# Early values loads, copies behind the products, and the MLP's first step ahead of the last early chunk

## The chip, the cores and the metric

One core of one Trainium2 chip runs the whole program. The metric is the device time of one execution in microseconds (us); less is better. The times shown are the median of three runs, and one further execution was taken with the hardware profiler.

## The reference

A gated linear attention feeds two MLPs one after the other. Cut to what matters:

```python
for t in range(S):                       # B=4, H=8, S=768, D=48
    state = alpha[:, :, t, :, None] * state + einsum('bhd,bhe->bhde', k[:, :, t], v[:, :, t])
    y[:, :, t] = einsum('bhd,bhde->bhe', q[:, :, t], state)
x = y.transpose(0, 2, 1, 3).reshape(B * S, H * D)      # 3072 x 384
x = silu(x @ w_in) @ w_out                             # 384 -> 2048 -> 384
out = (silu(x @ w_gate) * (x @ w_val)) @ w2_out        # 384 -> 1536 -> 384
```

The weights come as 64-bit floats; the kernel decodes them to 32 bits on the chip.

## The kernel before, in words

**Attention by chunks.** The sequence is cut into 24 chunks of 128 tokens (NCH; chunk n is batch n % 4, position n // 4), each with 8 heads in four pairs. Two pairs are a "duo" d, so chunk n has duos 2n and 2n+1. For a chunk VectorE runs a scan over the decays (`scan_r`, line 418), a reciprocal and a second scan (`scan_g`, line 431); GpSimd multiplies keys and queries by them (line 443, two products per chunk, named kq); TensorE makes the scores (`scores2`, line 455); VectorE masks them (`mask2`, line 469, into one of three `pt` buffers), ScalarE copies the keys (`keys2`, line 476); and TensorE makes the values product `pv` (line 638). For the first four chunks (n < NE = 4) `pv` has a second kind of matmul (line 659), which reads a rearranged copy of the values, `v3`, that lies in the tile `start`; `spread` (line 682, the copy on line 686) writes it on GpSimd. There are two such copies, used in turn.

**Early chunks.** Chunks 0 to 6 (NF = 7) are done by `early(m)` (line 482). Its calls set the order on each engine, which is the order in the program: scores of chunk m, `pv` of chunk m-1, masks and keys of chunk m, `chunk_high(m - 1)`, `spread(m)`, the scans and products of chunk m+2, from chunk 3 on a weight unit decoded by VectorE in a PSUM bank (`early_unit`, line 381), `chunk_end(m - 1)`, guards (squares summed on ScalarE, line 579), and loads of raw weights. Loads are issued on SP: `scan_g` ends with the load of the input of two chunks on, `chunk_end` with the values load `load_v(n + 2)` (line 405; two buffers). Fillers (line 609) are matmuls into a bank that nobody reads.

**The first MLP by blocks.** Tokens form seven blocks; block 0 is chunks 0 to 3 (512 columns), block 1 chunks 4 to 6 (384 columns). A step (j, f) of block j has a first-layer product `g1` (line 828, nine matmuls, with weight unit 2f), the Silu on ScalarE and a subtraction for the low part on VectorE (`act1`, line 835), and a second-layer product `g2` (line 855, unit 2f+1). Every unit is split into a high part (ScalarE, line 804) and a low part (VectorE, `sub`, line 322), since each product is made from high and low parts. Units 4 and on are decoded by `units1` (line 1372) in three VectorE instructions (lines 93, 98, 103) that are called between the steps. The list `turns` (line 1446) interleaves the steps of blocks 0 and 1; the main loop (line 1557) issues `g1` of step s+1 ahead of `g2` of step s. Ahead of it stand the last `pv` (chunk 6, `attn(1, False)`, line 1549), `open_late` (line 346: memsets on GpSimd and four copies on ScalarE, lines 351 to 360), the first `g1` and its Silu.

```python
        if m:
            pv(m - 1)
...
        if m < NE:
            spread(m)
        if m + 2 < NF:
            scan_r(m + 2, 0, NP)
            scan_g(m + 2, 0, NP)
```

After the first MLP (blocks 2 to 6 carry the other chunks' attention along) the second MLP follows; the change does not touch it.

Of the kernel before, what the change touches and what calls it, by code (L numbers as in the profile page):

```python
# [23 lines left out]
NCH = B * NC  # L24
# [244 lines left out]
def fast(ctx, tc, pk, w1, w2, out, bad_i):  # L269
# [5 lines left out]
    blocks1, n = [], 0  # L275
# [91 lines left out]
    in_t, raw_in, v_t, r_t = {}, {}, {}, {}  # L367
# [4 lines left out]
    NE, NF = B, len(blocks1[0]) + len(blocks1[1])  # L372
# [30 lines left out]
            load_in(later_in.pop(0)[1])  # L403

    def load_v(n):
        if n >= NCH:
            return
        v_t[n] = ap.tile([128, NP, C], F32, tag="in_v", name=f"in_v{n}")
        SP.dma_start(
            out=v_t[n], in_=pk[n, :, A_W + 2 * W:].rearrange("p (r e) -> p r e", r=NP)  # L410
        )
# [19 lines left out]
    def scan_g(n, i, k):  # L431


        rg, cs = rg4[n % 2], slice(i * CA, (i + k) * CA)
        DVE.tensor_tensor_scan(
            out=rg[:, 1, cs], data0=in_t[n][0][:, cs],
            data1=rc4[:, i:i + k].rearrange("p i t -> p (i t)"), initial=0.0, op0=ALU.mult, op1=ALU.add,
        )
        by_pair = rg.rearrange("p x (i t) -> p x i t", i=NP)
        for lo in range(i, i + k, 2):  # L440
            d = (n * NP + lo) // 2
            kq_t[d] = kqs[d % 6]
            (DVE if d == 0 else POOL).tensor_tensor(
                out=kq_t[d][:, :, :2 * C].rearrange("p i (x t) -> p x i t", x=2),
                in0=in_t[n][1][:, :, lo:lo + 2], in1=by_pair[:, :, lo:lo + 2, 1:], op=ALU.mult,
            )
        c, b = divmod(n, B)
        if c:
            for p in range(i, i + k):
                t = state[b][:, p]  # L450
                ACT.activation(out=t, in_=t, func=AF.Copy, scale=by_pair[:, 0, p, 0:1])
        if i + k == NP:
            load_in(n + 2)
# [28 lines left out]
    def early(m):  # L482

        if m == 0:
            yd_place(0)
        s = {}
        for d in (2 * m, 2 * m + 1):
            filler(max(m - 1, 0), 4 if d == 1 else 1)  # L490
            s[d] = scores2(d)
        if m:
            pv(m - 1)
        for d in s:
            mask2(d, s[d])
            keys2(d, s[d])
            if m == 0:
                (scan_r if d == 0 else scan_g)(1, 0, NP)
        if m:
            chunk_high(m - 1)  # L500
            yd_place(m)
        if m < NE:
            spread(m)
        if m + 2 < NF:
            scan_r(m + 2, 0, NP)
            scan_g(m + 2, 0, NP)
        if m >= 3:
            early_unit(yd_t[m][:, 512:])
        if m:
            chunk_end(m - 1)  # L510
        up_to("gd", 2 * m, guard, ND)
        up_to("l1", 2 * m + 1, load1, NU1)
# [91 lines left out]
    def yd_place(n):  # L604

        t = yd_t[n] = banks((6, 2)[(NF - 1 - n) % 2] if n < NF else 6, f"yd{n}")
        y_t[n] = t[:, 256:768]
# [30 lines left out]
    def pv(n):  # L638

        c, b = divmod(n, B)
        v = v_t[n]
        if n >= NF:
            yd_place(n)
        y = y_t[n]
        first, last = n * NP, n * NP + NP
        heads = [(p, h, slice(64 * h, 64 * h + 64)) for p in range(NP) for h in range(2)]
        pts = [pt_t.pop(g) for g in range(first, last)]
        for p, h, hs in heads:  # L650
            if n < NE and p == 0:
                continue
            cs, r = slice(p * C, p * C + C), half(p, h)
            PE.matmul(  # L654
                y[r:r + 64, cs], v[:, p, hs], pts[p][:, h], start=p in (n < NE, 2), stop=True,
                skip_group_check=True,
            )
            if n < NE:
                PE.matmul(
                    y[r:r + 64, cs], v3[n % 2][:, p - 1, hs], pts[0][:, h], start=False, stop=True,  # L660
                    skip_group_check=True,
                )
        if c < NC - 1:
            ds = ds_t[n] = yd_t[n][:, 768:768 + NP * D].rearrange("p (r e) -> p r e", r=NP)
            for p, h, hs in heads:
                PE.matmul(
                    ds[hs, p], kt_t[first + p][:, hs], v[:, p, 64 * h:64 * h + D],
                    start=False, stop=True, skip_group_check=True,
                )
            for g in range(first, last):  # L670
                kt_t.pop(g)
        if c:
            for p, h, hs in (heads[2 * p + h] for p in (0, 2, 1, 3) for h in range(2)):
                r = half(p, h)
                PE.matmul(
                    y[r:r + D, p * C:p * C + C], state[b][hs, p],
                    kq_t[(first + p) // 2][(hs, p % 2, slice(C, 2 * C)) if n < NF else (hs, 1, p % 2)],
                    start=False, stop=True,
                    skip_group_check=True,
                )  # L680

    def spread(n):


        t = v3[n % 2].rearrange("p k (h x) -> p k h x", h=2)
        POOL.tensor_copy(
            t[:, :, :, D:],
            v_t[n][:, 0].rearrange("p (h x) -> p h x", h=2)[:, :, :D].rearrange(
                "p h (k r) -> p k h r", k=KT
            ),  # L690
        )
# [136 lines left out]
    def g1(s):  # L828
        j, f = steps[s]
        w = len(blocks1[j]) * C  # L830
        h_t[j, f] = bank(s % 2, f"h{j}_{f}")[:, :w]
        xk = [(x_t[j][:, 0, k, :w], x_t[j][:, 1, k, :w]) for k in range(KT)]
        product(h_t[j, f], unit_t["1", 2 * f], xk)
# [494 lines left out]
    def attn(lag=1, more=True, first=None):  # L1328
        done, new = st["pv"], None
        if st["qk"] - st["pv"] * NP >= NP + lag - 1:  # L1330
            pv(done)
            st["pv"] += 1
        if more and st["qk"] < NG:
            new = st["qk"]
            qkt(new)
            st["qk"] += 1
        rest = first and first()
        if new is not None:
            d, odd = divmod(new, 2)
            ahead, top = d + 3, ND  # L1340
            causal(new)
            keys(new)
        if rest:
            rest()

        if st["pv"] > done:
            chunk_high(done)
            chunk_end(done)
        if new is None:
            return  # L1350
        if odd:
            up_to("a3", ahead, stage_a3, top)
            up_to("b", d + 2, stage_b, ND)
        else:
            up_to("a1", ahead, stage_a1, top)
            up_to("c", d + 1, stage_c, ND)
            up_to("a2", ahead, stage_a2, top)
            up_to("gd", d - 1, guard, ND)
        begin_later()
# [12 lines left out]
    def units1(ahead=4, top=NU1):  # L1372

        up_to("s1", st["h1"] - 1, lambda u: low_unit(("1", u), DVE), NU1)
        up_to("h1", st["f1"] - 1, lambda u: high_unit(("1", u), wp, "w"), NU1)
        up_to("e1", st["d1"] - 1, lambda u: decode_unit(("1", u), 1), NU1)
        up_to("d1", st["d1"], lambda u: decode_unit(("1", u), 0), min(top, st["l1"]))
        up_to("f1", st["e1"] - 1, lambda u: decode_unit(("1", u), 2), NU1)
        up_to("l1", st["d1"] + ahead - 1, load1, NU1)
# [63 lines left out]


    FB = 8
    turns = [(0, 0), (0, 1)]
    for k, n in enumerate((2, 2, 2, 2, 3, 3, 2)):
        f1 = sum(j for j, _ in turns)
        turns += [(1, f1 + i) for i in range(n)] + [(0, k + 2)] * (k + 2 < FB)
    steps = turns + [(0, f) for f in range(FB, NF1)]  # L1450
    steps += [(j, f) for j in range(2, NB1) for f in range(NF1)]

    due, n = [first] * (2 * len(turns)), first
# [92 lines left out]
    first_d = first // 2  # L1546
    need1(1)
    units1()
    attn(1, False)
    up_to("gd", first_d - 1, guard, ND)  # L1550
    estack.close()
    open_late()
    g1(0)
    rest = act1(*steps[0])
    units1()
    rest()
    for s, (j, f) in enumerate(steps):
        need1(2 * f + 1)
        if s == 0:
            units1()  # L1560
        n = 19 + 2 * (s + 3 - len(steps))
        if s + 1 < len(steps):
            need1(2 * steps[s + 1][1])
            if n >= 19:
                run(OUTPUT[n] - PAIR)
            g1(s + 1)
        slot(s, 0, (lambda: act1(*steps[s + 1])) if s + 1 < len(steps) else None)
        if n >= 19:
            if s + 1 < len(steps):
                free_banks.append((s + 1) % 2)  # L1570
            run(OUTPUT[min(n + 1, 23)] - PAIR)
        g2(j, f)
        slot(s, 1)

    wstack.close()
    free_banks += [2, 3, 4]
# [90 lines left out]
```

## Time and profile before

| | us |
|---|---|
| Median of 3 runs | 943.12 |
| Lowest and highest run | 943.05, 945.03 |
| The profiled execution's own time | 947.71 |
| Its span in the trace | 946.0 |
| TensorE (PE) busy | 905.8 (96%) |
| VectorE (DVE) busy | 611.6 (65%) |
| ScalarE (ACT) busy | 451.4 (48%) |
| GpSimd (POOL) busy | 279.4 (30%) |

The span is what the trace covers; the execution's own time has 1.7 us around it, and stands 4.6 us above the median of the runs without a profile. Busy shares are means over the whole span. SP issues most of the transfers, and SPq, ACTq are the queues' issues. PEld is TensorE's loading of weights, which overlaps its matmuls.

### The profile page before, as it was taken

The page shows a single profiled execution, that of the slowest core. Times are in us where ns is not written, and L with a number is a line of the kernel's source. Part 1 is how long each engine was busy: PE and PEld are TensorE (multiplying, and loading weights), DVE is VectorE, ACT ScalarE, POOL GpSimd, SP SyncE. Part 2 cuts the span into 40 slices and gives each one's busy share as a digit, 9 for nine tenths or more (in the row PEclk, how much of TensorE's full clock was granted, in tenths as well). Part 3 has the DMA queues.
Part 4 walks back from the last instruction along what each step waited for, and adds up shares of the span by engine and source line. Part 5 has one row for each costly group of instructions (what it writes and reads, how often), then busy time and mean ns, then how long its engine had stood idle before and what let it go on. Part 6 is the DMA issues. An engine that isn't in the chain of part 4 may idle for free.

```text
span 946.0 us, 14403 instructions
## 1 busy us (share of the span) xinstructions
PE 905.8 (96%) x5261; PEld 771.9 (82%) x5261; DVE 611.6 (65%) x1079; ACT 451.4 (48%) x1005; POOL 279.4 (30%) x389
## 2 busy tenths in 40 slices
PE   7569999999999999999999999999999999999996
PEld 4458998889999998888888888878888878888785
DVE  7569966556767577466258457786467875577732
ACT  1355544555556465455446444453454444444432
POOL 5311004528868789677318200000000000000000
PEclk8789999999999999999999999999999999999998
DMA  6665301233564465542466466632557513855301
GB/s 214 203 216 200 118 1 66 84 124 116 181 205 143 155 198 169 177 131 103 134 220 226 173 234 224 242 117 84 201 211 284 188 34 118 283 180 220 134 1 70
DMA packets 43007, 150.89 MB, mean 160 GB/s; under 512 B 4400, under 2 KB 9008, under 8 KB 40240
## 3 DMA queue, kind: packets, MB, share of 16 engines
q1 hardware_dynamic: 42304, 149.30, 46.3%
q8 instruction: 43, 0.70, 0.3%
q10 hardware_dynamic: 624, 0.59, 0.2%
q14 instruction: 36, 0.29, 0.1%
HBM read 118.03 MB, written 29.88 MB: 156 GB/s over the span
## 4 chain that ended last, share of the span: by engine, by line
PE 86%; DVE 3%; issue 3%; DMA 2%; POOL 2%; ACT 2%; SPq 1%; ACTq 0%; POOLq 0%
PE o L1257 15%; PE h L823 6%; PE x L872 6%; PE x L873 6%; PE x L875 6%; PE h L824 6%; PE h L826 6%; PE D L1194 5%; PE A L1194 5%; PE E L1194 5%; PE yd L654 3%; PE K L1194 2%; PE B L1194 2%; PE G L1194 2%; PE H L1194 2%
## 5 line engine op out<-in xcount | busy, mean ns | idle before, releaser
L322 DVE TENSOR_TENSOR gl<-h,gh 128x384 fp32r<-128x384 f32 (+1 forms) x112 | 68.5, 612 | 90.9 <-ACT h L841 85.6
L872 PE MATMUL x<-gh,w 128*128 128x384 f32 (+1 forms) x336 | 121.2, 361 | 4.3 <-DVE x1e L881 2.2
L823 PE MATMUL h<-x,w 128*128 128x384 f32 (+1 forms) x336 | 122.6, 365 | 1.8 <-DMA x<-y 1.6
L873 PE MATMUL x<-gh,w 128*128 128x384 f32 (+1 forms) x336 | 120.8, 360 | 0.0
L824 PE MATMUL h<-x,w 128*128 128x384 f32 (+1 forms) x336 | 120.8, 359 | 0.0
L840 ACT ACTIVATE gh<-h 128x384 fp32r<-128x384 f32 (+1 forms) x112 | 59.9, 535 | 101.1 <-PE h L826 99.7
L1257 PE MATMUL o<-gh,ring 128*128 128x512 f32 x288 | 88.7, 389 | 0.0
L875 PE MATMUL x<-gl,w 128*128 128x384 f32 (+1 forms) x336 | 84.5, 359 | 0.0
L826 PE MATMUL h<-x,w 128*128 128x384 f32 (+1 forms) x336 | 84.3, 358 | 0.0
L872 PEld LDWEIGHTS x<-gh,w 128*128 128x128 f32 x336 | 63.1, 188 | 10.6 <-DVE x1e L881 2.7
L823 PEld LDWEIGHTS h<-x,w 128*128 128x128 f32 x336 | 63.1, 188 | 10.6 <-issue 5.4
L531 POOL TENSOR_TENSOR kq<-in,r 128x256 f32<-128x256 f32 x34 | 33.7, 990 | 118.6 <-DVE r L520 118.6
L873 PEld LDWEIGHTS x<-gh,w 128*128 128x128 f32 x336 | 63.1, 188 | 5.2
L824 PEld LDWEIGHTS h<-x,w 128*128 128x128 f32 x336 | 63.1, 188 | 5.0
L875 PEld LDWEIGHTS x<-gl,w 128*128 128x128 f32 x336 | 61.4, 188 | 6.0 <-DVE gl L322 0.2
L826 PEld LDWEIGHTS h<-x,w 128*128 128x128 f32 x336 | 61.4, 188 | 5.9
L1257 PEld LDWEIGHTS o<-gh,ring 128*128 128x128 f32 x288 | 54.1, 188 | 11.2
L841 ACT ACTIVATE h<-h 128x384 f32<-128x384 f32 (+1 forms) x112 | 59.6, 533 | 0.0
L1257 PE MATMUL o<-gl,ring 128*128 128x512 f32 x144 | 56.4, 392 | 0.8 <-DVE gl L322 0.8
L322 DVE TENSOR_TENSOR gl<-a,gh 128x512 fp32r<-128x512 f32 x48 | 32.8, 691 | 37.3 <-ACT gh L1246 36.2
L1194 PE MATMUL A<-mov,ring 128*128 128x512 f32 x198 | 55.6, 389 | 0.0
L1194 PE MATMUL D<-mov,ring 128*128 128x512 f32 x198 | 55.6, 389 | 0.0
(219 smaller groups left out, 1951.8 us busy)
## 6 DMA issues: line engine op xcount, KB each, us to landing
ring<-comb_d SPq DMA_DIRECT2D x21, 1920.0 KB, 7.7
raw<-in_w_dram SPq DMA_DIRECT2D x58, 384.0 KB, 4.4
in<-in_pk_dram SPq DMA_DIRECT2D x22, 770.5 KB, 4.4
ring<-wo_d SPq DMA_DIRECT2D x6, 1920.0 KB, 7.4
comb_d<-area SPq DMA_DIRECT2D x8, 896.0 KB, 4.9
in_v<-in_pk_dram SPq DMA_DIRECT2D x24, 256.0 KB, 3.9
comb_d<-area SPq DMA_DIRECT2D x8, 640.0 KB, 5.1
x1r<-x_d SPq DMA_DIRECT2D x6, 768.0 KB, 8.9
```

The lines of the kernel that those rows point to most:

```text
L322: eng.tensor_tensor(out=lo, in0=src, in1=hi.bitcast(F32), op=ALU.subtract)
L531: POOL.tensor_tensor(out=kq_t[d][:, 0], in0=in_t[n][1][:, 0, ps_], in1=r_t[d][:, :, 1:], op=ALU.mult)
L823: PE.matmul(acc, part(u, k), xh, start=(k == 0), stop=False)
L824: PE.matmul(acc, part(u, k, 1), xh, start=False, stop=False)
L826: PE.matmul(acc, part(u, k), xl, start=False, stop=(k == len(xk) - 1))
L840: ACT.activation(out=gh, in_=hb, func=AF.Silu)
L841: ACT.activation(out=hb, in_=hb, func=AF.Silu)
L872: PE.matmul(x1_t[j][m], part(u, m), gh, start=(f == 0), stop=False)
L873: PE.matmul(x1_t[j][m], part(u, m, 1), gh, start=False, stop=False)
L875: PE.matmul(x1_t[j][m], part(u, m), gl, start=False, stop=(f == NF1 - 1))
L1194: PE.matmul(acc, s(hs, r), x[:, hx], start=op in new and i == 0, stop=i == 2, skip_group_check=True,)
L1257: PE.matmul(o_t[b][m], part(ring_t[p, f], m, l), x, start=(f == 0 and i == 0), stop=(f == NF2 - 1 and i == 2),)
```

## The change

The values load of chunk m+1 is issued in `early(m)` right behind `pv(m - 1)`, where it was the end of `chunk_end(m - 1)`; a second call for the same chunk does nothing. `spread(m)` stands behind the scans and products of chunk m+2. The list `turns` begins with three steps of block 0 instead of two, and block 0 stays one step further ahead. The first `g1` and its Silu stand ahead of the last early chunk's `pv`. `open_late` is called after step 2 of the main loop.

```diff
     def load_v(n):
-        if n >= NCH:
+        if n >= NCH or n in v_t:
             return
...
         if m:
             pv(m - 1)
+            load_v(m + 1)
...
-        if m < NE:
-            spread(m)
         if m + 2 < NF:
             scan_r(m + 2, 0, NP)
             scan_g(m + 2, 0, NP)
+        if m < NE:
+            spread(m)
...
-    turns = [(0, 0), (0, 1)]
+    turns = [(0, 0), (0, 1), (0, 2)]
     for k, n in enumerate((2, 2, 2, 2, 3, 3, 2)):
         f1 = sum(j for j, _ in turns)
-        turns += [(1, f1 + i) for i in range(n)] + [(0, k + 2)] * (k + 2 < FB)
+        turns += [(1, f1 + i) for i in range(n)] + [(0, k + 3)] * (k + 3 < FB)
...
     units1()
+    g1(0)
+    act1(*steps[0])()
     attn(1, False)
     up_to("gd", first_d - 1, guard, ND)
     estack.close()
-    open_late()
-    g1(0)
-    rest = act1(*steps[0])
     units1()
-    rest()
...
         g2(j, f)
         slot(s, 1)
+        if s == 2:
+            open_late()
```

How the instructions stand now. First GpSimd, early chunks; kq are the products, `start` holds the copies, in_v the values. Before:

```order
L443 TENSOR_TENSOR kq2_119<-in1_131,rg1_116 128x2x2x128
L443 TENSOR_TENSOR kq3_120<-in1_131,rg1_116 128x2x2x128
L686 COPY start_123<-in_v0_135 128x6x16
L443 TENSOR_TENSOR kq4_121<-in2_190,rg0_115 128x2x2x128
L443 TENSOR_TENSOR kq5_122<-in2_190,rg0_115 128x2x2x128
L686 COPY start_123<-in_v1_139 128x6x16
L443 TENSOR_TENSOR kq0_117<-in3_227,rg1_116 128x2x2x128
```

And with the change (line numbers behind line 494 are one higher):

```order
L443 TENSOR_TENSOR kq2_119<-in1_131,rg1_116 128x2x2x128
L443 TENSOR_TENSOR kq3_120<-in1_131,rg1_116 128x2x2x128
L443 TENSOR_TENSOR kq4_121<-in2_190,rg0_115 128x2x2x128
L443 TENSOR_TENSOR kq5_122<-in2_190,rg0_115 128x2x2x128
L687 COPY start_123<-in_v0_135 128x6x16
L443 TENSOR_TENSOR kq0_117<-in3_227,rg1_116 128x2x2x128
L443 TENSOR_TENSOR kq1_118<-in3_227,rg1_116 128x2x2x128
L687 COPY start_123<-in_v1_139 128x6x16
```

Each copy has moved behind the two products of the chunk two further on.

Then TensorE at the end of the early chunks, one row of each product (yd6 is chunk 6's values product, h0_1 the first-layer product of step (0, 1), x1_0 the second-layer product of block 0, w1_4 weight unit 4). Before:

```order
L675 MATMUL yd5_575<-kq5_122,state1_106 48x128 x2
L654 MATMUL yd6_645<-pt12_638,in_v6_586 64x128 x4
...
L823 MATMUL h0_0_730<-x0_284,w1_0_507 128x512
...
L823 MATMUL h0_1_756<-x0_284,w1_2_647 128x512
...
L872 MATMUL x1_0_778<-gh0_0_740,w1_1_577 128x512
...
L823 MATMUL h1_0_796<-x1_572,w1_0_507 128x384
```

With the change:

```order
L676 MATMUL yd5_577<-kq5_122,state1_106 48x128 x2
L824 MATMUL h0_0_673<-x0_286,w1_0_509 128x512
...
L655 MATMUL yd6_647<-pt12_640,in_v6_566 64x128 x4
...
L824 MATMUL h0_1_740<-x0_286,w1_2_649 128x512
...
L873 MATMUL x1_0_762<-gh0_0_683,w1_1_579 128x512
...
L824 MATMUL h0_2_780<-x0_286,w1_4_734 128x512
```

The first product has moved ahead of chunk 6, and the third product is one of block 0 with unit 4, where it was one of block 1 with unit 0.

Last VectorE at the same place, from unit 4's first decode step to its low part (y3_1 and x1 are chunk 6's end, gl the low part of an activation, raw1_4 and dec1_4 unit 4 in decoding). With the change:

```order
L93 TENSOR_SCALAR dec1_4_671<-raw1_4_371 128x384
L322 TENSOR_TENSOR gl0_0_684<-h0_0_673,gh0_0_683 128x512
L322 TENSOR_TENSOR y3_1_575<-yd6_647,y3_1_575 128x128
L322 TENSOR_TENSOR x1_574<-yd6_647,x1_574 48x3x128 x2
L745 TENSOR_TENSOR state2_107<-yd6_647,state2_107 128x192
L322 TENSOR_TENSOR w1_3_669<-raw1_3_303,w1_3_669 128x384
L98 SCALAR_TENSOR_TENSOR raw1_4_371<-raw1_4_371,dec1_4_671 128x384
L93 TENSOR_SCALAR dec1_5_731<-raw1_5_373 128x384
L103 SCALAR_TENSOR_TENSOR raw1_4_371<-raw1_4_371 128x384
...
L322 TENSOR_TENSOR gl0_1_751<-h0_1_740,gh0_1_750 128x512
L322 TENSOR_TENSOR w1_4_734<-raw1_4_371,w1_4_734 128x384
```

Here only gl0_0 has moved: before it stood behind unit 4's third decode step (line 103).

## Rows read from the trace of the kernel before

**Rows 1.** The page's first line: the span.

```profile
span 946.0 us, 14403 instructions
```

**Rows 2.** Stretches: from:to, length, then busy us per engine, granted clock, DMA.

```profile
0.00:63.40 63.40, 42.24 (x509) 27.12 (x509) 40.43 (x63) 21.00 (x68) 21.67 (x37) 0.78 0.66 216
63.40:75.60 12.20, 8.64 (x79) 6.95 (x76) 9.06 (x20) 8.72 (x27) 2.92 (x5) 1.00 0.62 188
75.60:160.00 84.40, 84.40 (x438) 77.94 (x437) 67.94 (x144) 39.35 (x84) 6.54 (x11) 1.00 0.28 94
```

**Rows 3.** Waits, 0 to 80 us: total us, times, longest.

```profile
PE yd L613 <- DVE raw L103: 10.7, 3, 4.7
```

**Rows 4.** Timeline of TensorE, early chunks: start us, us, what, [idle before <-releaser].

```profile
17.28 0.65 PE L659 MATMUL yd<-pt,start 128*64 128x128 f32 x4
...
21.93 0.32 PE L659 MATMUL yd<-pt,start 128*64 128x128 f32 x1
...
23.08 0.44 PE L659 MATMUL yd<-pt,start 128*64 128x128 f32 x4
...
31.79 0.90 PE L654 MATMUL yd<-pt,in_v 128*64 128x128 f32 x3 [1.32 <-DMA in_v<-in_pk_dram]
32.27 0.63 PE L659 MATMUL yd<-pt,start 128*64 128x128 f32 x2
...
40.20 0.58 PE L613 MATMUL yd<-mask 128*128 128x512 bf16 x1 [4.49 <-DVE raw L103]
```

**Rows 5.** Timeline of GpSimd, early chunks.

```profile
14.52 0.26 POOL L686 COPY start<-in_v 128x96 f32<-128x96 f32 x1
18.41 2.32 POOL L443 TENSOR_TENSOR kq<-in,rg 128x512 f32<-128x512 f32 x2 [3.63 <-DVE rg L435]
...
31.90 0.26 POOL L686 COPY start<-in_v 128x96 f32<-128x96 f32 x1 [6.04 <-DMA in_v<-in_pk_dram]
32.12 2.32 POOL L443 TENSOR_TENSOR kq<-in,rg 128x512 f32<-128x512 f32 x2
```

**Rows 6.** Timeline of VectorE, early chunks: masks (L474) and a scan (L435).

```profile
19.07 0.69 DVE L474 TENSOR_TENSOR pt<-s,mask 128x512 f32<-128x512 f32 x1 [0.17 <-PE yd L659]
...
23.67 1.28 DVE L474 TENSOR_TENSOR pt<-s,mask 128x512 f32<-128x512 f32 x2
...
35.09 0.69 DVE L474 TENSOR_TENSOR pt<-s,mask 128x512 f32<-128x512 f32 x1 [5.62 <-PE yd L654]
...
37.18 1.23 DVE L435 TENSOR_TENSOR_SCAN rg<-in,rc 128x516 f32<-128x516 f32 x1
```

**Rows 7.** Stretches behind two idle times of TensorE, as rows 2.

```profile
40.20:45.20 5.00, 5.00 (x45) 2.96 (x47) 1.01 (x2) 2.00 (x6) 2.54 (x3) 0.50 0.46 156
...
73.40:78.00 4.60, 4.55 (x22) 4.03 (x23) 4.12 (x10) 2.48 (x5) 0.19 (x2) 1.00 0.99 354
```

**Rows 8.** Timelines of TensorE, VectorE and GpSimd at the seam to the MLP.

```profile
64.93 1.09 PE L654 MATMUL yd<-pt,in_v 128*64 128x128 f32 x16 [1.49 <-issue]
...
66.99 0.50 PE L823 MATMUL h<-x,w 128*128 128x512 f32 x1
...
73.45 0.50 PE L872 MATMUL x<-gh,w 128*128 128x512 f32 x1 [2.07 <-ACT gh L840]
...
75.63 0.33 PE L823 MATMUL h<-x,w 128*128 128x384 f32 x1
...
69.44 1.12 DVE L322 TENSOR_TENSOR x<-yd,x 48x384 fp32r<-48x384 f32 x2 [1.35 <-ACT x L737]
...
71.91 1.13 DVE L93 TENSOR_SCALAR dec<-raw 128x384 int32<-128x384 int32 x1
...
75.11 0.36 DVE L93 TENSOR_SCALAR dec<-raw 128x384 int32<-128x384 int32 x1
...
76.46 0.55 DVE L322 TENSOR_TENSOR w<-raw,w 128x384 fp32r<-128x384 f32 x1
...
71.88 0.95 POOL L351 MEMSET ql<- 128x1024 f32 x1
```

## The prediction

> **What bounds the kernel now.** I read first the span [rows 1] and the stretch table [rows 2]. The program has three parts that matter here: the early chunks (0 to 63.4 us, TensorE 42.24 of 63.40 us busy at a mean granted clock of 0.78), the seam to the MLP (63.4 to 75.6 us, 8.64 of 12.20 busy), and from 75.6 us on a TensorE that does not pause (84.40 of 84.40 busy up to 160 us). In that third part VectorE is busy for 67.94 of 84.40 us, because it decodes the weights. So a microsecond lost or won before 75.6 us is passed on to the end nearly whole; behind it nothing stands that would take it up. The change lies wholly in front of, or just behind, that point.
>
> Then the waits of the first 80 us [rows 3] and the timelines of TensorE, GpSimd and VectorE [rows 4 to 6]. The early chunks go round a ring: TensorE's values product of chunk m-1 ends, VectorE's second mask of chunk m may then overwrite the score tile, VectorE scans chunk m+2 behind it, decodes a weight unit from chunk 3 on, and TensorE's next filler waits for that decode (10.7 us over three times, [rows 3]). The masks that wait start at 19.07, about 24.3 (the second of the pair at 23.67) and 35.09 us [rows 6]. The long step, 24.3 to 35.09, is due to the values of chunk 2, which TensorE waits for until 31.79 [rows 4] and GpSimd, which wants to copy them, for 6.04 us until 31.90; GpSimd's products of chunk 4 stand behind that copy until 32.12 [rows 5].
>
> **The values' load and the copy (one term).** The load of chunk m+1's values now goes out behind the values product of chunk m-1 ahead of one input load. That ends the wait at 31.79. But the copy also moves behind GpSimd's two products of chunk m+2, and the second kind of values product (line 659, 660 after the change) reads this copy for chunks 0 to 3. That closes a new ring: mask 2m+1, two scans, two GpSimd products, copy m, values product m, mask 2m+3. Worked out from rows:
> - Copy 0 was done at 14.52 + 0.26 = 14.8 us, before its reader at 17.28 [rows 4, 5]. Now it follows the products that begin at 18.41 and take 2.31: 20.73, and 0.26 for the copy, so 21.0 us. TensorE stands at 17.3 us for some 4 us.
> - From the first reader of the copy to the waiting mask: 21.93 to 23.08 + 0.44 = 1.6 us at full clock, and 32.27 to 35.09 = 2.8 us in the slow stretch [rows 4, 6].
> - From the mask to the next copy's reader: mask start to the end of the second scan 37.18 + 1.23 - 35.09 = 3.3, products 2.32, copy 0.26 [rows 5, 6], hand-overs about 0.15: 6.05 us in all.
> - So mask 3 starts at 21.0 + 2.8 = 23.8 (before 19.07), its next reader runs at 29.9, mask 5 at 31.5 (before 24.3), the next reader at 37.5, mask 7 at 39.8 (before 35.09). I take the slow 2.8 for the first, since TensorE idled for 4 us; 1.6 for the second (idle about 2.4 us); 2.3, midway, for the third (idle about 3 us).
> - With all three fast, mask 7 starts at 37.9, with all three slow at 41.6. **Term 1: 4.7 us later, ends 2.8 and 6.5.**
>
> What would hide it: nothing, since mask 7, the scans behind it and the decode that the filler waits for at 40.20 are one line on VectorE. From chunk 3 on the ring is as before; copy 3 would end at 39.8 + 6.0 = 45.8 at the latest; its reader stands behind the decode that the filler waits for (40.20 before, so about 45 now), that filler, another and two groups of scores, so I count no fourth wait. The queue of SP: the values of chunk 2 go out when chunk 0's product is done, at about 24.5, and are needed at 37.5; the input load of chunk 5 behind them waits for the products of chunk 3, goes out at about 29.6 and is needed by the scan at 40.4. Eleven and thirteen microseconds are there for each, so moving the loads costs nothing and, with the copy where it is, also wins nothing.
>
> **The MLP's first step ahead of the last early chunk, and three steps of block 0 (two terms).** TensorE idled 1.49 us before 64.93 and 2.07 before 73.45 [rows 8]. The first product of the MLP (2.2 us, as 75.63 - 73.45) now starts when chunk 5's values product ends, at 64.93 - 1.49 = 63.4; chunk 6's (66.99 - 64.93 = 2.1) ends at 67.7, the second product at 69.9, and the first second-layer product at 72.0 instead of 75.63, all in the time scale of the kernel before. That fills both gaps, 3.6 us. But the next product is now step (0, 2), which needs weight unit 4, where before it was step (1, 0), which needs unit 0. Unit 4's low part ran at 76.46 + 0.55 = 77.0 [rows 8] and nobody was waiting for it, since two steps of block 1 came first. Does VectorE reach it earlier now? Chunk 6's last subtractions (69.44 before) come about 1.3 us later, because the two Silu of the first step stand ahead of them on ScalarE; the first low part of the activation (0.6 us and 0.4 of waiting) leaves the line behind them; and the decode step that took 1.13 us beside GpSimd's memset, where 0.36 is usual [rows 8], is the question. The memset itself is coded later, but GpSimd has nothing ahead of it, so it runs when the last guard on ScalarE frees its memory, about 1.3 us later than before; its second piece, at 71.88 before [rows 8], then begins at about 73.2, and that is also where the decode step now falls.
>
> [...]
>
> So unit 4 is whole at 76.8 (no meeting) to 77.6 us (meeting, which I take). TensorE idles from 72.0, for one matmul only at about 75. At 77.6 it has done what it had done at 75.63 and one matmul of 0.23 more: **Term 2: 1.8 us, ends 1.0 and 1.8.**
>
> **Term 3, the clock after that idle.** [...] Five us at half clock do the work of 2.5: **2.5 us, ends 0 and 2.5.** [...]
>
> The later parts: the order of the remaining steps only lets block 0 lead by one more, with the same 24 steps; each of block 1's new units is wanted one step later, which eases VectorE. The four ScalarE copies into the query tile (0.8 us) now stand in the middle of the steps; ScalarE is busy for 39.35 of 84.40 us there [rows 2]. Both at nothing; if that cover is gone, 0.8 us.
>
> **Sum.** 4.7 + 1.8 + 2.5 = 9.0 us. It is made against the profiled execution (947.71 us, span 946.0), which stands 4.6 us above the median of 943.12; a difference made in the first 85 us carries over unchanged, so 943.1 + 9.0 = 952.1. The low ends give 2.8 + 1.0 = 3.8 (946.9), the high ends 6.5 + 1.8 + 2.5 + 0.8 = 11.6 (954.7).
>
> **Rivals.**
> - Clock stays up (chance 0.20): the one matmul at 75 us keeps it. Then 4.7 + 1.8 = 6.5: 949.6. For it speaks that 2.07 us of idle did no harm, against it the 4.49 us.
> - The copy holds nobody, and the early load wins (chance 0.07), the case on the faster side. Its place is the step from mask 5 to mask 7, its price 24.3 to 35.09 = 10.8 us now against 5.2 for the step before it (19.07 to 24.3): 5.5 us gained, less term 2, so 943.1 - 5.5 + 1.8 = 939.4. It decides at one point: whether copy m ends before its first reader comes to it. For it speaks the 6.04 us that GpSimd waited for the values [rows 5]; against it, that the products ahead of copy 0 cannot begin before 18.41, and its reader stood ready at 17.28.
> - The two cancel (chance 0.08): the ring costs its low end and a part of the early stretch comes back at the seam, because unit 4 is there by 73 to 74; about 943 to 945. Against it: unit 4's decode stands behind chunk 6's end on VectorE.
> - VectorE falls behind (chance 0.07): while TensorE runs slow, VectorE waits for its products, and decoding (busy 67.94 of 84.40 us, and without a pause at its beginning) becomes the bound later; 2 to 4 us more, 955 to 956.
> - My forecast, with all three terms: 0.58.
>
> **How the numbers follow.** Smallest difference that a measurement of this kernel can tell: 0.2%, 1.9 us. Slower by more: forecast, first and last rival, 0.85. Within it 0.08, faster 0.07. The range leaves out the faster case, a part of the cancelling one and the last: 945.8 to 955.0.
>
> **What would show it.** In the changed kernel's timeline: the first copy on GpSimd at about 20.7 us instead of 14.52; TensorE waiting for GpSimd's copies at line 660 three times, about 9 us together; the waiting masks near 23.8, 31.5 and 39.8; no wait of GpSimd for the values; later one wait of TensorE of 4 to 6 us in a first-layer product for VectorE's low weights, with a granted clock near half behind it. I am wrong if mask 7 starts before 36 us, or if step (0, 2) starts without a wait.

## The result and the profile after

| | us |
|---|---|
| Changed kernel, median of 8 runs | 952.26 (951.71 to 955.65) |
| Kernel before, median of 8 runs beside it | 946.75 (943.05 to 949.63) |
| Ratio, 95% interval | 1.0069 [1.0043, 1.0095] |
| Profiled execution of the changed kernel, its span | 951.9, 949.9 |
| The same of the kernel before | 947.71, 946.0 |

The changed kernel is slower, by 4.1 to 9.0 us on the interval (0.7%). The predicted 952.1 us and its range hold the time. The difference is another matter: the forecast was +9.0 us on a base of 943.12, and the 8 runs of the kernel before have a median of 946.75. The forecast's three runs are among these 8; the other five lie at 944.60 to 949.63. Further sets of 35, 23 and 13 runs gave it 947.26, 946.52 and 948.15. One run of the kernel before (1020.82 us) and one of the kernel with the Silu behind (1816.46 us) lie far above all others and are in no comparison here. The three runs on which the forecast stood were at the low end, and measured side by side the change costs 5.5 us between the medians, 6.5 by the ratio. What follows asks of each term whether it had its size, and where the other microseconds went.

First the waits of the changed kernel up to 85 us (total us, times, longest):

```profile
PE yd L614 <- DVE raw L103: 10.4, 3, 4.7
...
PE yd L660 <- POOL start L687: 9.2, 3, 3.3
...
PE h L824 <- ACT w L805: 3.4, 1, 3.4
...
PE h L825 <- DVE w L322: 1.8, 1, 1.8
```

The first line is that of [rows 3], as large as before: the ring of decode and filler goes on. The other three are new. TensorE now waits three times for GpSimd's copy, 9.2 us in all ("about 9" in the prediction), and once, in two pieces of 3.4 and 1.8 us, for the high and the low part of weight unit 4. The copies and products on GpSimd, where [rows 5] had a copy at 14.52:

```profile
17.75 2.31 POOL L443 TENSOR_TENSOR kq<-in,rg 128x512 f32<-128x512 f32 x2 [3.21 <-DVE rg L435]
...
20.01 0.26 POOL L687 COPY start<-in_v 128x96 f32<-128x96 f32 x1
...
74.95 1.27 POOL L351 MEMSET qh<- 128x1408 f32 x1 [19.37 <-ACT jk L583]
...
76.16 0.95 POOL L351 MEMSET ql<- 128x1024 f32 x1
```

VectorE's waiting masks, to be held against [rows 6], and unit 4 at the seam, against [rows 8]:

```profile
23.20 0.69 DVE L474 TENSOR_TENSOR pt<-s,mask 128x512 f32<-128x512 f32 x1 [4.95 <-PE yd L660]
...
30.91 0.69 DVE L474 TENSOR_TENSOR pt<-s,mask 128x512 f32<-128x512 f32 x1 [3.35 <-PE yd L660]
...
39.20 0.69 DVE L474 TENSOR_TENSOR pt<-s,mask 128x512 f32<-128x512 f32 x1 [3.93 <-PE yd L655]
...
76.20 1.13 DVE L93 TENSOR_SCALAR dec<-raw 128x384 int32<-128x384 int32 x1
...
80.14 0.55 DVE L322 TENSOR_TENSOR w<-raw,w 128x384 fp32r<-128x384 f32 x1
```

And TensorE, whose rows at the seam were [rows 8]:

```profile
20.32 0.47 PE L660 MATMUL yd<-pt,start 128*64 128x128 f32 x1 [3.33 <-POOL start L687]
...
37.06 0.32 PE L660 MATMUL yd<-pt,start 128*64 128x128 f32 x1 [3.17 <-POOL start L687]
...
64.29 1.09 PE L655 MATMUL yd<-pt,in_v 128*64 128x128 f32 x16
...
66.35 0.50 PE L824 MATMUL h<-x,w 128*128 128x512 f32 x1
...
78.44 0.50 PE L824 MATMUL h<-x,w 128*128 128x512 f32 x1 [3.37 <-ACT w L805]
80.74 0.79 PE L825 MATMUL h<-x,w 128*128 128x512 f32 x1 [1.80 <-DVE w L322]
81.33 0.63 PE L824 MATMUL h<-x,w 128*128 128x512 f32 x1
...
164.32 0.32 PE L600 MATMUL s<-qh,kh 128*128 128x352 f32 x1
```

The copy is done at 20.27, the masks start at 23.20, 30.91 and 39.20 (forecast 21.0, 23.8, 31.5 and 39.8; in this execution the whole ring began some 0.7 us earlier). The first-layer product of step (0, 2) waits at 75 to 81 us, and a matmul that otherwise takes 0.39 us takes 0.63 behind it: half clock, as the stretch table says (third figure from the end):

```profile
80.00:85.00 5.00, 4.26 (x10) 3.39 (x11) 3.75 (x9) 1.00 (x2) 0.00 (x0) 0.50 1.02 398
```

**One table for all traces.** Two points on TensorE cut every trace into three parts: the start of chunk 5's values product (61.31 us before), with which the early chunks end, and the first scores product behind the seam (157.25 before), by which VectorE's decoding for blocks 0 and 1 is over. In the first profile of the kernel before they are:

```profile
61.31 1.09 PE L654 MATMUL yd<-pt,in_v 128*64 128x128 f32 x16
...
157.25 0.32 PE L599 MATMUL s<-qh,kh 128*128 128x352 f32 x1
```

The table gives how much later they start than there, their difference (what the seam costs), and the span's difference from 946.0. The kernels are explained below.

| kernel | chunk 5 | at 157 us | seam | span |
|---|---|---|---|---|
| changed | +2.98 | +7.07 | 4.09 | +3.9 |
| changed, again | +5.29 | +9.65 | 4.36 | +7.7 |
| before, again | -0.46 | -0.46 | 0.00 | +0.6 |
| early load alone | -4.76 | -4.78 | -0.02 | -6.5 |
| early load alone, again | -3.48 | -3.45 | 0.03 | -5.0 |
| copies behind, alone | +3.17 | +3.18 | 0.01 | +1.1 |
| copies back | -3.59 | +0.70 | 4.29 | -1.8 |
| two leads | +5.14 | +5.94 | 0.80 | +4.3 |
| copies back, two leads | -1.81 | -0.96 | 0.85 | -0.9 |
| the same, Silu behind | -5.87 | -5.84 | 0.03 | -6.2 |
| gap filled | +3.00 | +4.79 | 1.79 | +5.4 |
| gap filled, again | +4.96 | +6.74 | 1.78 | +7.4 |
| late memsets | +2.64 | +9.66 | 7.02 | +8.1 |

The seam repeats to some tenths from one execution to the next. The early chunks do not (2.98 and 5.29 for the same kernel), and neither does the part behind 157 us. There the first profile of the kernel before has three short waits of TensorE:

```profile
330.31 0.44 PE L872 MATMUL x<-gh,w 128*128 128x384 f32 x1 [0.85 <-DVE x1e L881]
...
345.93 0.43 PE L599 MATMUL s<-qh,kh 128*128 128x352 f32 x1 [0.33 <-ACT kt L633]
...
402.39 0.50 PE L872 MATMUL x<-gh,w 128*128 128x512 f32 x1 [1.37 <-DVE x1e L881]
```

A trace without them gains about 1.0, 0.5 and 1.6 us on it at these three places, and a trace in which the granted clock falls at one of two longer waits (last section) loses 1.2 to 1.6 us there. Both come and go in one and the same kernel: the kernel before has two of the three waits the second time, and the early load alone has two of them in one trace and none in the other. So the step from the column at 157 us to the span column tells of single executions, not of what an edit does.

### The profile page after: what moved, and what is told of

Its sections match the earlier page's. It is cut to its first block, busy times and chain, and to the rows that moved or that the text cites. A ratio compares the mean times of both kernels' runs of the same rounds, so it can differ in the third digit from the quotient of the medians.

```text
span 949.9 us, 14397 instructions
## 1 busy us (share of the span) xinstructions
PE 907.6 (96%) x5261; PEld 772.6 (81%) x5261; DVE 609.7 (64%) x1079; ACT 452.2 (48%) x1005; POOL 278.9 (29%) x389
## 4 chain that ended last, share of the span: by engine, by line
PE 90%; DVE 4%; issue 2%; DMA 1%; ACT 1%; POOL 1%; SPq 0%; ACTq 0%; POOLq 0%
PE o L1258 15%; PE h L824 7%; PE x L873 7%; PE h L825 7%; PE x L874 7%; PE h L827 7%; PE x L876 7%; PE D L1195 5%; PE A L1195 5%; PE E L1195 5%; PE yd L655 2%; PE K L1195 2%; PE B L1195 2%; PE G L1195 2%; PE H L1195 2%
```

## The experiments

**e3_load_only: the early load alone, on the kernel before.**

```diff
-        if n >= NCH:
+        if n >= NCH or n in v_t:
...
             pv(m - 1)
+            load_v(m + 1)
```

> The kernel before with the early values load alone (copy, MLP order and open_late as before). My theory: the load was the long pole of chunk 2 only by a little, so the mask that started at 35.09 us starts 1.3 to 3 us earlier, and the time is 1 to 3 us (0.1 to 0.3%) below the kernel before. Rival (the copy's place is harmless and the early load wins 5.5 us): 5 us or more below. Rival (the load is hidden anyway): no change, mask at 35 us.

Measured: 942.59 us against 947.26, ratio 0.9961 [0.9944, 0.9978]. Faster than both kernels. GpSimd's waits for the values, and VectorE's masks, in its trace:

```profile
26.07 0.61 POOL L687 COPY start<-in_v 128x96 f32<-128x96 f32 x1 [1.27 <-DMA in_v<-in_pk_dram]
...
33.16 0.36 POOL L687 COPY start<-in_v 128x96 f32<-128x96 f32 x1 [2.59 <-DMA in_v<-in_pk_dram]
```

```profile
23.94 0.69 DVE L474 TENSOR_TENSOR pt<-s,mask 128x512 f32<-128x512 f32 x1 [0.65 <-PE yd L660]
...
31.63 0.69 DVE L474 TENSOR_TENSOR pt<-s,mask 128x512 f32<-128x512 f32 x1 [2.48 <-PE yd L655]
```

The step from mask 5 to mask 7 is 7.7 us, where it was 10.8: the wait of 6.04 us for the values [rows 5] shrinks to 1.27, but is not gone. So the mechanism of the faster rival is real, 3.5 to 4.8 us of it at chunk 5 (its price had been put at 5.5, and I had expected 1 to 3 us here), and the changed kernel loses it.

**e4_copy_only: the copies behind the products, alone.**

```diff
-        if m < NE:
-            spread(m)
         if m + 2 < NF:
             scan_r(m + 2, 0, NP)
             scan_g(m + 2, 0, NP)
+        if m < NE:
+            spread(m)
```

> The kernel before with the copies behind GpSimd's products alone (loads and MLP order as before). My theory: the new ring costs all of the early stretch by itself: waiting masks near 23, 31 and 39 us, last waiting mask (62.02 before) near 65, and 3 to 4 us (0.3 to 0.4%) more than the kernel before. Rival (late copies only matter together with the MLP order): within 1 us of before.

Measured: 949.35, ratio 1.0033 [1.0016, 1.005]. Its trace has the same three waits for the copy (7.6 us in all) and chunk 5 comes 3.17 us later. The copies' place costs 3 us where the load is late, and more where it is early, as the next run shows.

**e1_copy_back: the changed kernel with the copies put back ahead** (the diff of e4 reversed).

> The changed kernel with the copies put back ahead of the products (early load, MLP order and open_late of the change). My theory: the early stretch ends 1 to 3 us earlier than in the kernel before, the seam still costs the wait for unit 4 and the slow clock behind it, 4.2 us: 1 to 3 us above the kernel before and 4 to 6 us below the changed one. Rival (the seam is free or wins): 1 to 4 us below the kernel before.

Measured: 946.19, ratio 0.9994 [0.9976, 1.0011], against 1.0069 of the changed kernel. The early chunks end 3.59 us earlier than before, then the seam costs 4.29 us. What the early load wins, the seam gives back. I had expected 1 to 3 us above the kernel before, since I gave the early load too little. Over all profiled executions, chunk 5 comes 2.64 to 5.29 us later with the copies behind (seven), and 1.81 to 5.87 us earlier with the early load and the copies in front (five).

**e2_two_leads: the changed kernel with two leading steps of block 0, as before.**

```diff
-    turns = [(0, 0), (0, 1), (0, 2)]
+    turns = [(0, 0), (0, 1)]
...
-        turns += [(1, f1 + i) for i in range(n)] + [(0, k + 3)] * (k + 3 < FB)
+        turns += [(1, f1 + i) for i in range(n)] + [(0, k + 2)] * (k + 2 < FB)
```

> The changed kernel with two leading steps of block 0 as before (copies behind, early load, first step ahead of chunk 6 as in the change). My theory: the early stretch stays 3 us late, but no wait for unit 4 and no half clock behind it; instead step (1, 0) waits 1 to 2 us for block 1's input. 2 to 4 us above the kernel before, 3 to 5 us below the changed one. Rival (the wait for unit 4 costs nothing, since VectorE sets the pace of the steps anyway): as the changed one.

Measured: 950.37, ratio 1.003 [1.0014, 1.0046]. The wait for unit 4 is gone, and with it 3.3 to 3.6 us of the seam (0.80 where 4.09 and 4.36 stood). The third leading step is what makes the seam expensive; in the medians it is worth 0.2 to 0.4% here (1.003 against 1.005 and 1.0069).

**e5_copy_back_two: copies back and two leads together**, so that the early load and the first step ahead of chunk 6 remain.

> The changed kernel with the copies put back ahead of the products and with two leading steps of block 0, so that the early load, the first step ahead of chunk 6 and the later open_late remain. My theory: the early load wins 3 to 4 us as it did in the run of that load alone, step (0, 2) comes late enough for unit 4, and the first step ahead of chunk 6 fills the two gaps at the seam of 1.5 and 2.1 us at most: median 2.5 to 6 us below the kernel before, ratio 0.994 to 0.997, no wait of a first-layer product for unit 4. Rival: the first step ahead of chunk 6 loses by itself, since its Silu delays chunk 6's end on ScalarE and VectorE; then the ratio is about 1.000, as in the run with the copies back and three leading steps.

Measured: 945.44, ratio 0.9991 [0.9975, 1.0007]. My expectation missed: I had counted on the two filled gaps. TensorE's two waits at the seam do shrink, from 1.49 and 2.07 us [rows 8] to 0.48 (for chunk 6's end, ahead of the first product of block 1) and 1.18 (for the Silu of the second step), and still the seam costs 0.85. VectorE shows why: counted from chunk 5's product, its last decode step stands 0.84 us later than in the kernel before (0.79 in the run with two leads, where the seam costs 0.80), and TensorE follows it.

The rival's ratio came true. Of its cause, the first step ahead of chunk 6, these 0.85 us are shown. The run is some 3 us slower than the early load alone (945.44 and 942.59); where the rest is lost is not shown, and `open_late`, which also stands later here, was not tried by itself. Beside the run with the copies back, the third lead costs only 0.03% of the time here, though 3.4 us at 157 us; why the medians do not show these 3.4 us stays open too.

**e8_silu_behind: the same, with the first step's Silu behind chunk 6's values product.**

```diff
     g1(0)
-    act1(*steps[0])()
     attn(1, False)
+    rest = act1(*steps[0])
     up_to("gd", first_d - 1, guard, ND)
     estack.close()
+    rest()
     units1()
```

> As the run with copies back and two leading steps, but the Silu of the first step stands behind chunk 6's end, as in the kernel before, while its product stays ahead of chunk 6's values product. My theory: the two Silu in front delay chunk 6's end on ScalarE by about 1.1 us; behind it, chunk 6's end and step (1, 0) come 1 us earlier, and the time is 0 to 2 us below that run's. Rival: the first second-layer product, which waits for the Silu, comes later by the same amount: no difference, or up to 1 us slower.

Measured: 945.21, ratio 0.9984 [0.9967, 1.0001], by the intervals not told apart from the run before. Its trace is worth more than its time. One early product of block 1 and VectorE's last decode step, in this kernel and in that with the early load alone:

```profile
72.67 0.69 PE L827 MATMUL h<-x,w 128*128 128x384 f32 x3
...
124.19 0.56 DVE L103 SCALAR_TENSOR_TENSOR late<-late 128x384 int32<-128x384 int32 x1
```

```profile
75.60 0.68 PE L827 MATMUL h<-x,w 128*128 128x384 f32 x3
...
125.25 0.56 DVE L103 SCALAR_TENSOR_TENSOR late<-late 128x384 int32<-128x384 int32 x1
```

At this product the kernel is 2.93 us ahead, of which 1.11 come from the early chunks (-5.87 against -4.76); 1.82 us were won at the seam. At 157 us nothing of them is left: the seam column says 0.03. In between VectorE has no time to spare; this stretch of the same kernel shows it (third busy figure):

```profile
90.00:100.00 10.00, 10.00 (x54) 9.08 (x52) 9.83 (x23) 4.74 (x11) 0.00 (x0) 1.00 0.36 99
```

VectorE is busy for 9.83 of 10 us, in the kernel before too (9.86). A gap filled on TensorE alone lets VectorE decode no sooner: its last decode step is 1.06 us ahead (124.19 against 125.25), no more than the early chunks gave it. So TensorE's 1.82 us are handed back step by step until that decoding ends. The microseconds won in the early chunks, where VectorE's work also moves forward, stayed (5.87 at chunk 5, 5.84 at 157 us).

**e7_fill_gap and f2_fill_again: the changed kernel with 22 fillers in front of step (0, 2).**

```diff
+            if s == 1:
+                wide = mask.rearrange("p (o t) -> p o t", o=1).to_broadcast([128, 4, C])
+                keep = bank(5, "keep").rearrange("p (o t) -> p o t", o=4)
+                for _ in range(22):
+                    PE.matmul(keep, mask, wide, start=True, stop=True)
             g1(s + 1)
```

> The changed kernel with 22 more filler matmuls (four columns blocks of the mask, into a bank that nobody reads) ahead of the first-layer product of step (0, 2), where TensorE waits 3.4 and 1.8 us for unit 4. Adds matmuls whose result nobody uses. My theory (third term): TensorE's granted clock stays at 1.00 behind the place, so that the stretch of about 5 us at half clock goes: 2 to 2.5 us less than the changed kernel, ratio 1.004 to 1.005 against the kernel before. Rival: the clock is not what the wait costs, or the decode of the next units on VectorE paces the stretch: same time as the changed kernel, 1.007, with VectorE waited for a little later.

Measured: 955.06, ratio 1.0096 [1.0076, 1.0116], slower than the changed kernel, where 2 to 2.5 us less was expected. At the place itself the theory holds. TensorE in this trace, and the stretch:

```profile
74.93 4.92 PE L1569 MATMUL keep<-mask 128*128 128x512 bf16 x22
...
80.75 0.50 PE L825 MATMUL h<-x,w 128*128 128x512 f32 x1 [0.67 <-DVE w L322]
81.09 0.40 PE L824 MATMUL h<-x,w 128*128 128x512 f32 x1
```

```profile
80.00:85.00 5.00, 4.33 (x20) 3.56 (x20) 4.74 (x11) 2.11 (x4) 0.00 (x0) 1.00 1.02 401
...
203.00:208.00 5.00, 4.53 (x15) 3.57 (x16) 0.75 (x2) 0.87 (x2) 0.00 (x0) 0.73 0.28 76
```

Unit 4 is there at the same time (80.75 and 80.74), the granted clock is 1.00 instead of 0.50, and the seam costs 1.79 instead of 4.09 us. The second line shows where 1.56 us of that went: behind a wait of 1.69 us for a transfer, at 203 us, the clock falls to 0.73, as it did not in the changed kernel's trace. I ran both again side by side.

> The changed kernel with the 22 fillers ahead of step (0, 2), again. Its first trace was 2.3 us ahead of the changed kernel's up to 190 us, yet its runs were slower. Theory: the 2.3 us are real and the rest is what the clock and VectorE do behind 190 us, which differs from execution to execution, so that its median now stands within 2 us of the changed kernel's, on either side. Rival: the fillers make a later part worse every time, by 2 to 5 us: ratio 1.009 again, and the trace shows the same lost places as the first (near 204 us and near 337 us).

> The changed kernel unchanged, in the same comparison as the next two. Median 951 to 954, ratio 1.005 to 1.008. In its trace the wait for unit 4 and the half clock behind it stand as before; behind 190 us the clock may fall or not at the two waits of 1.6 and 2.0 us, for a transfer and for ScalarE.

Measured: with the fillers 956.13, ratio 1.0085 [1.0062, 1.0107]; the changed kernel 952.5, ratio 1.005 [1.0029, 1.007]. The rival came closer: the fillers win 2.3 to 2.6 us at the seam, both traces lose 1.5 to 1.6 at the wait near 203 to 205 us, and the runs are some 3 us slower all the same. Of the two lost places that the rival named, the second, a wait of 1.31 us for VectorE at 337.50 us, stands in the first trace only. The second trace is even 0.3 us shorter than the changed kernel's beside it (spans of 953.4 and 953.7), so the traces do not show the 3 us. Why the clock falls near 204 us in both traces with fillers, in neither of the changed kernel and in one of the ten others (the kernel before, again), and where the 3 us go, stays open.

**f4_late_memset: the memsets held back until step 12.**

```diff
-        if s == 2:
-            open_late()
+        if s == 12:
+            open_late(act_t[j, f][0])
...
+            if name == "qh":
+                POOL.tensor_copy(late_t[name][:, 0, :16], behind[:, :16])
             POOL.memset(late_t[name].bitcast(F32), 0.0)
```

> The changed kernel with its late memsets on GpSimd held back: a GpSimd copy of 16 columns of step 12's activation stands ahead of them, and the four ScalarE copies follow, so that no memset runs beside the decode of unit 4. Reading it from the trace, not from the time. My theory (the 0.8 us in the second term): the decode step that took 1.13 us takes 0.36, unit 4's low part runs 0.8 us earlier against chunk 5's values product, and the wait of the first-layer product for it shrinks from 1.8 to about 1.0. Rival: the memset is only beside it; the decode of unit 4 waits for something else ahead and the low part stands where it stood (15.85 us behind the start of chunk 5's values product).

VectorE and then TensorE in its trace, one execution (956.0 us):

```profile
75.85 0.36 DVE L93 TENSOR_SCALAR dec<-raw 128x384 int32<-128x384 int32 x1
...
79.02 0.55 DVE L322 TENSOR_TENSOR w<-raw,w 128x384 fp32r<-128x384 f32 x1
```

```profile
77.32 0.50 PE L826 MATMUL h<-x,w 128*128 128x512 f32 x1 [2.60 <-ACT w L807]
79.62 0.80 PE L827 MATMUL h<-x,w 128*128 128x512 f32 x1 [1.80 <-DVE w L322]
```

Without the memset beside it the decode step takes 0.36 instead of 1.13 us. The low part stands 15.07 us behind chunk 5's product (63.95 here) instead of 15.85, and the wait shrinks from 3.37 + 1.80 to 2.60 + 1.80. That the first piece shrinks and not the second, as I had expected, is no contradiction: the wait for the high part ends with the same decode (in the changed kernel ScalarE waits 2.98 us for VectorE's line 103 before it makes that part). So the 0.8 us are shown at this place; how much of them would be left at 157 us this trace cannot say. By time the edit is no remedy: the load of a later weight group, which comes behind step 12 then, goes out on SP at 128.16 instead of 111.18 us, and VectorE waits 3.11 us for it.

**e0_before: the kernel before, profiled once more.**

> The kernel before, profiled a second time. The profiled execution shown of it had three short waits of TensorE behind 320 us (0.85, 0.33 and 1.37 us, for activations and for VectorE), which the changed kernel's had not. My theory: these differ from execution to execution of the same kernel, so that here they stand at other places or have another sum (0 to 4 us in all), while everything ahead of 320 us stands within 1 us of the first profile. Rival: they belong to the kernel: the same three waits at the same places within 0.3 us.

Measured: ahead of 157 us it stands 0.46 us from the first profile at both points of the table. Behind it two of the first profile's three waits are there (0.72 and 0.33 us), and that of 1.37 us at 402 is not. The theory held, and showed something larger, which the section on the hardware tells.

**f3_load_again: the early load alone, again.**

> The kernel before with the early load of the values alone, again, since it was the fastest. Theory: 3 to 5 us faster than before, ratio 0.995 to 0.997. Rival: its gain was a lucky set of executions: ratio 0.998 or more.

Measured: 942.68 against 948.15, ratio 0.9944 [0.9923, 0.9965]. The gain repeats. This is the version to keep.

## Why the prediction was right, point by point

- **The new ring.** Right in kind and nearly in time: three waits for the copy, masks 0.6 us ahead of the forecast each. Of the 4.7 us, mask 7 shows 4.11 (39.20 against 35.09). The sentence "from chunk 3 on the ring is as before" was too simple. Up to chunk 5's product the delay became 2.98 us in one execution and 5.29 in the next (the seven executions with the copies behind fall into two groups, 2.64 to 3.17 and 4.96 to 5.29), along with the granted clock (third figure from the end), which is lower in the second of them in both stretches. The kernel before, the changed kernel, and the changed kernel again:

```profile
45.00:55.00 10.00, 5.35 (x68) 3.47 (x65) 5.98 (x9) 4.36 (x14) 2.32 (x2) 0.67 0.59 210
55.00:60.00 5.00, 3.46 (x73) 2.66 (x65) 3.29 (x7) 1.82 (x7) 0.00 (x0) 0.92 0.98 295
```

```profile
45.00:55.00 10.00, 5.35 (x74) 3.53 (x73) 5.84 (x9) 4.03 (x13) 2.01 (x4) 0.84 0.57 185
55.00:60.00 5.00, 5.00 (x70) 3.17 (x70) 1.65 (x4) 2.13 (x7) 0.59 (x1) 0.66 0.68 196
```

```profile
45.00:55.00 10.00, 6.88 (x74) 4.72 (x74) 4.49 (x7) 4.36 (x14) 0.98 (x2) 0.67 0.56 185
55.00:60.00 5.00, 3.43 (x34) 1.80 (x34) 2.51 (x5) 2.11 (x6) 2.32 (x2) 0.50 0.31 98
```

  The bounds of 2.8 and 6.5 hold six of the seven executions with the copies behind (2.64 to 5.29).
- **The early load, which "with the copy where it is, also wins nothing".** The runs agree: copies behind give 1.0033 [1.0016, 1.005] without it, and 1.003 [1.0014, 1.0046] with it and the two-lead seam; at chunk 5 the delay is 3.17 us without it and 2.64 to 5.29 with it.
- **The seam's wait.** Forecast 1.8 us, shown 1.79 and 1.78 (in the two traces with fillers, where a matmul behind the wait takes 0.39 to 0.40 us and not 0.63), with the 0.8 us of the memset's neighbourhood in it (0.77 and 0.78 by the wait and by the low part's place). The same decode instruction took 1.13 us with the memset beside it (76.20 us in the changed kernel) and 0.36 without (75.85 in f4); what in the memset makes the difference no run here shows.
- **The clock behind the wait.** Forecast 2.5 us, shown 2.30 and 2.58 (4.09 - 1.79 and 4.36 - 1.78). The 5 us at half clock were my estimate from [rows 4] and [rows 7]: 0.50 for 5.00 us behind an idle time of 4.49 us, and 1.00 behind one of 2.07. The changed kernel's clock was 0.50 from 80 to 85 us, behind its waits of 3.37 and 1.80; with fillers in the wait it was 1.00 in that stretch of the first trace. What in the idle time decides the clock no run here shows. The rival in which the clock stays up did not come true: the granted clock was 0.50.
- **"A difference made in the first 85 us carries over unchanged."** As a rule this failed: the 1.82 us that the run with the Silu behind won on TensorE at the seam alone were lost again by 157 us, when VectorE's decoding is over (seam column 0.03), and "behind it nothing stands that would take it up" left out that VectorE paces that stretch (busy for 9.83 of 10 us). For the changed kernel it held part of the way. From 157 to 320 us the delay stands still to 0.1 us (7.07 to 7.06); then the trace makes up 3.2 us, all at the three waits which the first profile of the kernel before has and this one has not. The second trace makes up 1.9, the same 3.2 less a fall of the clock. As such waits come and go in one kernel, this does not show that a delay is taken up. Forecast and traces agree at 157 us (9.0 against 7.07 and 9.65); that the medians differ by less, 5.5 us, stays open in part.
- **The base.** 943.12 from three runs was some 3.5 us low. That the predicted time is right to 0.2 us is luck: a base that was too low and a difference that was some 3 us too large (9.0 against 5.5 to 6.5) cancelled one another.

## What to carry to other kernels

Ask of every microsecond won whether the engine that paces the next stretch also gets it: an earlier load moved the whole ring, VectorE included, and was kept; a filled gap on TensorE was not. When a helper's copy is moved behind larger work on its engine, follow it to its reader, since here that alone turned chunk 5's lead of 3.9 us into a delay of 3.9 (means of the five and of the seven traces). And test the parts of a bundle one by one: the one edit worth keeping, 0.4 to 0.6% by itself, was hidden by the others.

## What the runs showed of the hardware that was not expected

The same idle time did not always cost the clock. Every trace has a wait of TensorE of 1.6 us near 200 us and one of 2.0 us near 367 us. The kernel before met them in two executions with the following clocks (third figure from the end), first its first profile, with the two waits:

```profile
198.57 0.41 PE L823 MATMUL h<-x,w 128*128 128x384 f32 x1 [1.63 <-DMA x<-y]
...
367.28 0.43 PE L599 MATMUL s<-qh,kh 128*128 128x352 f32 x1 [2.04 <-ACT kt L633]
...
200.00:205.00 5.00, 5.00 (x27) 4.60 (x27) 1.25 (x2) 2.34 (x5) 0.00 (x0) 1.00 0.10 32
...
368.00:373.00 5.00, 5.00 (x65) 4.51 (x65) 3.50 (x8) 2.57 (x8) 5.00 (x6) 1.00 0.72 277
```

and its second:

```profile
200.00:205.00 5.00, 5.00 (x21) 4.51 (x20) 1.17 (x2) 1.96 (x4) 0.00 (x0) 0.77 0.03 11
...
368.00:373.00 5.00, 4.91 (x36) 4.47 (x38) 3.75 (x8) 2.68 (x9) 4.92 (x5) 0.66 0.77 263
```

In the first the clock stays at 1.00 behind both, in the second it falls behind both, and the execution loses 1.4 us at the one and 1.5 at the other. Over all 14 traces it falls behind the first wait in three and behind the second in eight. What decides it the traces do not show. The clock goes along with the spread of 943 to 950 us that this kernel's runs have: over 35 of them span and mean granted clock (0.979 to 0.989) have a correlation of -0.73; how much of that falls at these two waits and how much in the early chunks the runs do not tell. So a single trace of a kernel with such waits says where time is lost at a place, and not by how much two kernels differ at the end.
